# Attention with a split exponential: zeros counted by streaming time, doubled waves, GpSimd's lag in the plan, v in 22 columns

## The chip, the cores and the metric

The kernel runs on one core of a Trainium2 chip. A core has five engines that each run their own instruction list in order: TensorE (PE, matrix products), VectorE (DVE), ScalarE (ACT), GpSimd (POOL) and SyncE (SP, which starts transfers). They meet only at semaphores. TensorE writes its results to PSUM, in banks of 128 x 512 float32; everything else lies in SBUF. The metric is the device time of one execution in microseconds.

## The reference

Softmax attention over 32 heads of 2,048 rows and 20 columns, with normalised queries and keys and a temperature for each head:

```python
def reference(q, k, v, t):
    eps = 1e-6
    qn = q / (jnp.sqrt((q * q).sum(axis=-1, keepdims=True)) + eps)
    kn = k / (jnp.sqrt((k * k).sum(axis=-1, keepdims=True)) + eps)
    logits = jnp.einsum('bhqd,bhkd->bhqk', qn, kn) * t[None, :, None, None]
    attn = _softmax(logits, axis=-1)
    return jnp.einsum('bhqk,bhkd->bhqd', attn, v)
```

q, k and v are [1, 32, 2048, 20] in bf16, t is [32]. The logits are bounded by t, so the kernel takes no maximum: it sums exp(logit) times v and, in one more column of ones, exp(logit) itself, and divides at the end.

## The kernel before

**Tiling.** The heads are taken in 8 groups of 4 (`NH`), each head of a group in its own strip of 32 rows of TensorE. A group has 4 blocks of 512 queries (`QW`), so there are 32 blocks (`NSB`). In a block each of the 4 heads has 16 pieces of 128 keys: 64 units of 128 keys x 512 queries, 2,048 units in all. A unit is one matmul of kT against qT, an exponential of 128 x 512, and one or more matmuls of the result against v that add into `psO`, where head hh owns the partitions 32·hh to 32·hh + 31. Four heads use four strips, so up to four of these small matmuls run at once.

**Two paths for the exponential.** On the first path a wave of two units goes to one of two slots of `psA`, ScalarE computes exp on 128 x 1024 (L885), and each unit costs one product with v (`vaug`). On the second path a unit goes to one of three banks of `psD`. VectorE turns it into 16-bit integers that are the bits of an approximate power of two (`P1`, L325, into `dI`). Two more terms come from adding a constant to those integers: the shifts (`dS1`, `dS2`), on GpSimd (L338, two 16-bit numbers in one int32) or on VectorE (L340). The three terms, with the first one taken against v and also against half of v (`vhalf`, made at L345), cost four products with v. `dI` and `dS` are rings of 24 units (`RING`).

**The plan.** The order of all engines is written by a planner in Python when the kernel is built (`make_plan`). It steps through time in steps of 0.005 us, gives every operation a cost and a latency, and lets each engine take its next piece of work by rules. The result is a fixed list for each engine, with the waits that the data need. The rules that the change touches:

- `step_pe0` puts a wave on `psA` as soon as its slot is free, and with it a wave on `psD` if banks are empty (`step_qkd`). Between waves it does products with v (`pv_round`). `ALONE`, `DJOIN`, `PVHOLD` hold work back when a slot comes free soon. `D_WAIT` holds the second path when too many shifts wait; `D_END` and `D_LAST` end it near the end of the last block or move it on from the end of another.
- While `psO` of a finished block is being drained (VectorE transposes it to `accT`, L360), no product with v can be issued. In that time a wave is issued three times over, to the same place, if TensorE has been used too little (L875). Elsewhere `step_heat` adds a matmul of zeros into `psO` (L558, `HEATN` = 128 columns). "Used" is `in_use`: the share of the last `HEATW` us, weighted by the share of the four strips in use, against `HEAT`. At the very start `HEAT0` zero matmuls of 512 columns run (L562).
- `step_dve` picks VectorE's next operation by priority; two neighbouring conversions become one of 1024 columns if at least `JOINB` shifts wait. `shift_run` gives VectorE up to four shifts in one operation.
- `step_pool` gives GpSimd work that fits under an operation of VectorE that doesn't use the port that the two share (conversions, drains, reductions), with up to `POOL_MAX` shifts in one operation and `PSLACK` us of overrun. It makes GpSimd wait for the operation of VectorE before that one. `lock` keeps VectorE's port operations (shifts, squares, scalings, the half copy) back until GpSimd is done in the plan.
- Loads and transposing transfers go through SP's queue (`load_qk`, `load_v`, `tr_op`) with planned latencies. `PREP1` spreads the preparation of the second head group over time, `LOAD1` says when its loads may start, `PREPW` weighs GpSimd's operations in that spread.
- `zeros` fills the padding columns of `kpad`, `qpad` and `vaug` on GpSimd at the start. v has 20 columns, one of ones, and zeros up to 32.

## Time and profile before

| | us |
|---|---|
| median of 3 runs | 632.83 |
| lowest, highest | 632.67, 633.11 |
| the profiled execution's own time | 633.45 |
| its span, first to last instruction | 631.5 |

In the profile PE is TensorE's matmul, PEld its weight load, and each group of instructions has its line, engine, operation, `out<-in`, how often, then busy time in us, the mean of one in ns, and how long the engine sat idle just before such instructions with what ended that. Matmuls are pipelined and up to four run at once, so PE's busy share is no measure of how full TensorE is. Means of single operations include the tail that the next one overlaps. The granted clock of TensorE is given as a share of full speed; over the execution it averaged 0.995.

### The profile page before, as it was taken

What the parts mean: (1) busy time and instruction counts of PE and PEld (TensorE: products, weight loads), DVE (VectorE), ACT (ScalarE), POOL (GpSimd) and SP (SyncE); (2) the same over time, 40 slices, a digit from 0 to 9 for tenths busy, and PEclk for the clock granted to TensorE, in tenths of its full rate; (3) what the DMA queues carried; (4) which work ended last, traced back from release to release, by engine and by line L of the source; (5) the groups of instructions that cost most, each with busy time, mean ns of one, the idle gap of its engine ahead of it and who ended that gap; (6) DMA issues with size and microseconds to landing.
All of it is one profiled execution on the core that took longest, in us unless ns stands there. A gap on an engine that the chain in (4) does not pass through costs nothing.

```text
span 631.5 us, 15864 instructions
## 1 busy us (share of the span) xinstructions
PE 614.5 (97%) x6794; PEld 180.3 (29%) x6794; DVE 614.1 (97%) x869; ACT 618.8 (98%) x675; POOL 445.5 (71%) x491
## 2 busy tenths in 40 slices
PE   8999999999999999999999999999999999999996
PEld 4432222322222232223223222232222332222221
DVE  6999999999999999999999999999999999999995
ACT  6999999999999999999999999999999999999995
POOL 4586667766677776876768666776777777666772
PEclk8999999999999999999999999999999999999999
DMA  6610404041040130306031050400404022010000
GB/s 73 88 10 16 95 1 43 2 62 48 2 43 2 35 76 5 39 2 111 1 29 16 1 110 3 40 4 3 93 3 57 2 33 37 1 23 6 6 5 13
DMA packets 113772, 19.57 MB, mean 31 GB/s; under 512 B 102944, under 2 KB 113696, under 8 KB 113696
## 3 DMA queue, kind: packets, MB, share of 16 engines
q1 hardware_dynamic: 112896, 18.37, 19.9%
q8 instruction: 55, 0.90, 0.6%
q10 hardware_dynamic: 800, 0.12, 0.1%
q14 instruction: 21, 0.17, 0.1%
HBM read 7.87 MB, written 2.62 MB: 17 GB/s over the span
## 4 chain that ended last, share of the span: by engine, by line
ACT 72%; PE 26%; DVE 1%; DMA 0%; issue 0%; POOL 0%
ACT pA L885 72%; PE psO L714 12%; PE psA L692 10%; PE psD L692 2%; PE psO L558 2%; DMA qk<-in_q_dram 0%; DVE ssum L263 0%; POOL kpad L304 0%; DVE accT L360 0%; PE psD L570 0%; DVE sqs L260 0%; DVE ost L368 0%; DVE qT L585 0%; DVE rn L289 0%; DVE rec L364 0%
## 5 line engine op out<-in xcount | busy, mean ns | idle before, releaser
L885 ACT ACTIVATE pA<-psA 128x1024 f16<-128x1024 f32 (+1 forms) x667 | 614.5, 1111 | 2.0 <-PE psA L692 1.6
L338 POOL TENSOR_TENSOR dS<-dI,shc 128x256 int32<-128x256 int32 (+2 forms) x378 | 373.0, 1007 | 130.0 <-DVE dS L340 93.2
L325 DVE TENSOR_SCALAR dI<-psD 128x1024 int16<-128x1024 f32 (+1 forms) x486 | 434.1, 927 | 4.4 <-PE psD L692 1.8
L692 PE MATMUL psA<-qT,kT 32*128 32x512 bf16 x1553 | 283.0, 384 | 8.9 <-ACT pA L885 6.0
L714 PE MATMUL psO<-pA,vaug 128*32 128x512 f16 (+1 forms) x1333 | 233.7, 384 | 0.0
L714 PE MATMUL psO<-dS,vaug 128*32 128x512 f16 x1430 | 224.5, 385 | 0.0
L692 PE MATMUL psD<-qT,kT 32*128 32x512 bf16 x715 | 193.9, 383 | 0.0
L714 PE MATMUL psO<-dI,vaug 128*32 128x512 f16 x715 | 155.3, 386 | 0.0
L714 PE MATMUL psO<-dI,vhalf 128*32 128x512 f16 x715 | 152.0, 384 | 0.0
L692 PEld LDWEIGHTS psA<-qT,kT 32*128 32x128 bf16 x1553 | 69.0, 91 | 239.4 <-ACT pA L885 224.1
L340 DVE TENSOR_SCALAR dS<-dI 128x2048 int16<-128x2048 int16 (+2 forms) x182 | 122.5, 679 | 0.0
L714 PEld LDWEIGHTS psO<-dS,vaug 128*32 128x32 bf16 x1430 | 51.1, 94 | 73.2 <-issue 58.7
L714 PEld LDWEIGHTS psO<-pA,vaug 128*32 128x32 bf16 x1333 | 52.5, 94 | 37.5 <-issue 31.8
L692 PEld LDWEIGHTS psD<-qT,kT 32*128 32x128 bf16 x715 | 45.4, 91 | 22.1 <-DVE dI L325 10.2
L714 PEld LDWEIGHTS psO<-dI,vaug 128*32 128x32 bf16 x715 | 36.7, 93 | 24.5 <-issue 17.4
L714 PEld LDWEIGHTS psO<-dI,vhalf 128*32 128x32 bf16 x715 | 36.4, 94 | 22.0 <-issue 19.2
L366 POOL TENSOR_TENSOR ost<-accT,rec 128x320 bf16<-128x320 f32 x31 | 23.3, 753 | 16.7 <-DVE dS L340 9.5
L304 POOL TENSOR_TENSOR qpad<-qk,rn 128x320 bf16<-128x320 bf16 x31 | 22.0, 728 | 17.3 <-DVE dS L340 10.4
L558 PE MATMUL psO<-zt 128*128 128x128 bf16 x310 | 32.3, 228 | 0.1
L304 POOL TENSOR_TENSOR kpad<-qk,rn 128x320 bf16<-128x320 bf16 x31 | 22.2, 738 | 10.8 <-DVE dS L340 6.1
L558 PEld LDWEIGHTS psO<-zt 128*128 128x128 bf16 x310 | 19.7, 101 | 21.0 <-issue 20.1
L360 DVE STREAM_TRANSPOSE accT<-psO 128x512 f32<-128x512 f32 x32 | 22.6, 705 | 2.7 <-PE psO L714 2.7
(51 smaller groups left out, 100.1 us busy)
## 6 DMA issues: line engine op xcount, KB each, us to landing
vaug<-in_v_dram SPq DMA_DIRECT2D x32, 80.0 KB, 4.0
qk<-in_k_dram SPq DMA_DIRECT2D x7, 320.0 KB, 4.0
out_dram<-ost SPq DMA_DIRECT2D x28, 80.0 KB, 1.9
qk<-in_q_dram SPq DMA_DIRECT2D x6, 320.0 KB, 3.9
qk<-in_q_dram SPq DMA_DIRECT2D x4, 80.0 KB, 3.1
out_dram<-ost SPq DMA_DIRECT2D x7, 40.0 KB, 2.0
qk<-in_k_dram SPq DMA_DIRECT2D x1, 240.0 KB, 3.6
qk<-in_q_dram SPq DMA_DIRECT2D x1, 240.0 KB, 4.2
```

Of the source, the lines that this page charges most:

```text
L304: emit = lambda e, o=dst, x=src, s=sc: e.tensor_tensor(o, x, s, ALU.mult)
L325: lambda e: e.tensor_scalar(dst, psD[:, pb * QW:(pb + n) * QW], 1024.0 * LOG2E, 15360.0 - 1024.0 * LOG2K + SHIFTS[0], ALU.mult, ALU.add),
L338: lambda e: e.tensor_tensor(o.bitcast(I32), x.bitcast(I32), c, ALU.add), rd + ["shc"], wr)
L340: lambda e: e.tensor_single_scalar(o, x, float(SHIFTS[i] - SHIFTS[0]), ALU.add), rd, wr)
L360: dve("drain", QW, R1, lambda e: e.transpose(aT[:, :, :].rearrange("p b d -> p (b d)"), psO[:, :]), ["psO"], [("accT", b)], 0.03),
L366: pool_op("omul", 320, True, lambda e: e.tensor_tensor(dst, num, rcb, ALU.mult), [("accT", b), ("rec", b)], [("ost", ob, qg)]) if pool else
L558: return lambda e: e.matmul(bank, zt[:, 0:128], zt[:, 0:n], start=False, stop=False, skip_group_check=True)
L692: return lambda e: e.matmul(dst, lhsT, rhs, tile_position=(32 * hh, 0))
L714: return lambda e: e.matmul(dst, lhsT, rhs, start=first, stop=last, skip_group_check=True, tile_position=(0, 32 * hh))
L885: a = Op("ACT", "exp", lambda e, s=src, d=dst: e.activation(d, s, ACT.Exp), [("psA", slot)], [("pA", pslot, i) for i in range(WAVES[slot]) ...
```

## The change

Four things in the planner and one in the data, with new values for its constants:

- `in_use` is now the share of time in which any matmul streams, overlaps counted once. Zeros are added below `HEAT` = 0.7 of the last 1.7 us (before: 0.57 of strip-weighted use in 3.41 us). In a drain a wave is issued twice (`TWICE`), not three times, if the share is below `HEATQ` = 0.8. `HEAT0` is 13, and its first matmul now writes all of `psO`.
- GpSimd's operation under a VectorE operation is planned to start `PLAG` after the end of the VectorE operation before it, and the port is planned free `LOCKL` before its end. Up to four shifts in one operation.
- The latencies of the first loads (`LOAD0`) and of the transposing transfers (`TRL`, `TRK`) are longer in the plan.
- `vaug` and `vhalf` have 22 columns for each piece, not 32, and the products with v write 22 partitions of each strip.

```diff
-D_END = 6
-D_LAST = 18
-D_WAIT = 36
+VW = 22
+D_END = 2
+D_LAST = 14
+D_WAIT = 30
-PREPW = 0.3
-PREP1 = (.25,.35)
+PREPW = 0.2
+PREP1 = (.15,.45)
-DFIRST = 1
+DFIRST = 2
-JOINB = 8
-POOL_MAX = 3
-ALONE = (.2, 0)
+JOINB = 12
+POOL_MAX = 4
+ALONE = (.2,.2)
-PVHOLD = (.22,.22)
-HEAT0 = 11
+PVHOLD = (.25,.25)
+HEAT0 = 13
-HEAT = .57
-HEATW = 3.41
+HEAT = 0.7
+HEATQ = 0.8
+TWICE = 2
+HEATW = 1.7
+LOAD0 = 2.75
+TRL = 2.25
+TRK = 1.2
+PLAG = .03
+LOCKL = 0.12
-PSLACK = 0.15
+PSLACK = 0.3
-SOON = 8
+SOON = 1.2
-LOAD1 = 0.2
-DJOIN = 0.3
+LOAD1 = 0
+DJOIN = 0.4
...
-        vaug = [sbuf(f"vaug{i}", [128, NH, R, 32], BF16) for i in range(2)]
+        vaug = [sbuf(f"vaug{i}", [128, NH, R, VW], BF16) for i in range(2)]
...
-            return dve("vh", NH * R * 32, R4, lambda e: e.tensor_single_scalar(f(vpart[c]), f(vaug), c, ALU.mult),
+            return dve("vh", NH * R * VW, R4, lambda e: e.tensor_single_scalar(f(vpart[c]), f(vaug), c, ALU.mult),
...
-                        0.5, 4.0 if part != 0 else 2.2)]
+                        0.5, 4.0 if part != 0 else LOAD0)]
...
-                       [(which + "pad", b, r) for r in range(r0, r1)], keys, 0.58 + 0.17 * (r1 - r0), 1.75 + 0.17 * (r1 - r0))
+                       [(which + "pad", b, r) for r in range(r0, r1)], keys, 0.58 + 0.17 * (r1 - r0), TRL + 0.17 * (r1 - r0) + TRK * (hg == 0 and which == "k"))
...
-            o = Op("PE", "heat", None, ["zt"], [("psA", 0)])
+            o = Op("PE", "heat", None, ["zt"], [("psA", 0), "psO"])
...
                 for hh in strips:
                     s0 = max(st, grp[hh])
                     grp[hh] = s0 + TS
+                    used_w.append((s0, s0 + TS))
                     end = max(end, grp[hh])
...
-                used_w.append((st, end, 0.25 * TS * len(strips) / (end - st)))
...
-                dst = psO[32 * hh:32 * hh + 32, :]
+                dst = psO[32 * hh:32 * hh + VW, :]
...
-                return sum(max(0.0, min(b, now) - max(a, t0)) * c for a, b, c in used_w) / HEATW
+
+                x, u = t0, 0.0
+                for a, b in sorted(used_w):
+                    a, b = max(a, x), min(b, now)
+                    if b > a:
+                        u, x = u + b - a, b
+                return u / HEATW
...
-                        if cur > 0 and not cur_free() and in_use() < HEAT:
-                            mms, st_ = mms * 3, st_ * 3
+                        if cur > 0 and not cur_free() and in_use() < HEATQ:
+                            mms, st_ = mms * TWICE, st_ * TWICE
...
-                fits = lambda c: not busy or now + c <= end + PSLACK
+                st = max(now, on[-2].done + SEML + PLAG) if busy and len(on) > 1 else now
+                fits = lambda c: not busy or st + c <= end + PSLACK
...
-                finish(o, now, o.cost, o.lat)
-                free_["POOL"] = lock[0] = now + o.cost
+                finish(o, st, o.cost, o.lat)
+                free_["POOL"], lock[0] = st + o.cost, st + o.cost - LOCKL
```

More of the change, by code (lines that the diff above doesn't have):

```diff
@@ L178, in bass_standalone__qk_norm__prompt_kernel @@
         kT = [sbuf(f"kT{i}", [128, S], BF16) for i in range(2)]
-        vaug = [sbuf(f"vaug{i}", [128, NH, R, 32], BF16) for i in range(2)]
-        vpart = {c: [sbuf(f"v{n}{i}", [128, NH, R, 32], BF16) for i in range(2)] for c, n in ((.5, "half"),)}
+        vaug = [sbuf(f"vaug{i}", [128, NH, R, VW], BF16) for i in range(2)]
+        vpart = {c: [sbuf(f"v{n}{i}", [128, NH, R, VW], BF16) for i in range(2)] for c, n in ((.5, "half"),)}
         pA = sbuf("pA", [128, NPA // 2 * sum(WAVES) * QW], BF16)
@@ L501, in zeros @@
                 return [z(kpad[i][:, :, :, D:32], 0.0, "kz"), z(qpad[i][:, :, :, D:32], 0.0, "qz"),
-                        z(vaug[i][:, :, :, D:D + 1], 1.0, "vz"), z(vaug[i][:, :, :, D + 1:32], 0.0, "vz")]
+                        z(vaug[i][:, :, :, D:D + 1], 1.0, "vz"), z(vaug[i][:, :, :, D + 1:VW], 0.0, "vz")]
             pool_init(0.2, [Op("POOL", "iota", lambda e: e.iota(iot[:, :], [[-1, 128]], base=0, channel_multiplier=1,
@@ L558, in heat_mm @@
                 return lambda e: e.matmul(bank, zt[:, 0:128], zt[:, 0:n], start=False, stop=False, skip_group_check=True)
-            o = Op("PE", "heat", None, ["zt"], [("psA", 0)])
-            o.info = [(lambda e, i=i: e.matmul(psA[:, (i % 3) * QW:(i % 3 + 1) * QW], zt[:, 0:128], zt[:, :])) for i in range(HEAT0)]
+            o = Op("PE", "heat", None, ["zt"], [("psA", 0), "psO"])
+            o.info = [lambda e: e.matmul(psO[:, :], zt[:, 0:128], zt[:, :])] + [(lambda e, i=i: e.matmul(psA[:, (i % 3) * QW:(i % 3 + 1) * QW], zt[:, 0:128], zt[:, :])) for i in range(HEAT0 - 1)]
             P.link(o)
@@ L565, in make_plan @@
             free_["PE"] = 0.5 + 0.427 * HEAT0
-            used_w = [(0.0, 0.0, 0.0)]
+            used_w = [(0.0, 0.0)]
             psQ = psD[:, QW:2 * QW]
@@ L679, in pe_put @@
                 if st - used_w[0][0] > 20:
-                    del used_w[0:20]
-                used_w.append((st, end, 0.25 * TS * len(strips) / (end - st)))
+                    del used_w[0:40]
                 op.start, op.done = st, end + PEL
@@ L815, in step_heat @@
                 pe_mode, pe_t = "heat", st + 0.02
-                used_w.append((st, st + n, 1.0))
+                used_w.append((st, st + n))
                 op.start, op.done = st, st + n + PEL
```

## The prediction

> **What bounds the kernel now.** I read the page first: the shares of the engines, the chain that ended last, the costliest groups.
>
> ```profile
> span 631.5 us, 15864 instructions
> ...
> PE 614.5 (97%) x6794; PEld 180.3 (29%) x6794; DVE 614.1 (97%) x869; ACT 618.8 (98%) x675; POOL 445.5 (71%) x491
> ...
> ACT 72%; PE 26%; DVE 1%; DMA 0%; issue 0%; POOL 0%
> ...
> L885 ACT ACTIVATE pA<-psA 128x1024 f16<-128x1024 f32 (+1 forms) x667 | 614.5, 1111 | 2.0 <-PE psA L692 1.6
> L338 POOL TENSOR_TENSOR dS<-dI,shc 128x256 int32<-128x256 int32 (+2 forms) x378 | 373.0, 1007 | 130.0 <-DVE dS L340 93.2
> L325 DVE TENSOR_SCALAR dI<-psD 128x1024 int16<-128x1024 f32 (+1 forms) x486 | 434.1, 927 | 4.4 <-PE psD L692 1.8
> L692 PE MATMUL psA<-qT,kT 32*128 32x512 bf16 x1553 | 283.0, 384 | 8.9 <-ACT pA L885 6.0
> L692 PE MATMUL psD<-qT,kT 32*128 32x512 bf16 x715 | 193.9, 383 | 0.0
> L340 DVE TENSOR_SCALAR dS<-dI 128x2048 int16<-128x2048 int16 (+2 forms) x182 | 122.5, 679 | 0.0
> L558 PE MATMUL psO<-zt 128*128 128x128 bf16 x310 | 32.3, 228 | 0.1
> ```
>
> ScalarE's 667 exponentials take 614.5 us and were kept waiting 2.0 us in all. That is 0.921 us for a wave of two units, 0.461 us a unit. The rest of the span is the start and the tail, so a faster TensorE alone has next to nothing to give: what counts is how many of the 2,048 units go to ScalarE. Now 715 go the other way (the psD matmuls), over VectorE and GpSimd. The view of the middle by windows says whether VectorE has room for more (columns: window, length, then busy time of PE, PEld, DVE, ACT, POOL, the granted clock, the DMA share, GB/s):
>
> ```profile
> 20.00:620.00 600.00, 591.63 (x6584) 169.87 (x6583) 595.82 (x818) 599.38 (x651) 436.20 (x474) 1.00 0.20 30
> ```
>
> It has not: VectorE idles 4.2 us of 600 and ScalarE 0.6 us. Two engines share the work and both are full, so a gain must come from VectorE time that falls away or goes to GpSimd, or from the two ends.
>
> **The exchange rate.** A unit on the second path costs VectorE 434.1/715 = 0.607 us for its conversion and 122.5/715 = 0.171 us for its share of the shifts, 0.778 us in all. If F us of VectorE time come free, x more units go there with 0.778x + 0.461x = F, and the time falls by 0.461x = 0.37 F. If both shifts of the added units fall on VectorE the rate is 0.33. I use 0.35. One unit that changes sides for any other reason is worth 0.46 us.
>
> **GpSimd's runs (POOL_MAX 3 to 4, PSLACK, PLAG, LOCKL).** By shape, and one cycle in order of time (start, length), with a place where GpSimd ran late:
>
> ```profile
> L325 DVE TENSOR_SCALAR dI<-psD 128x1024 int16<-128x1024 f32 x229 | 277.2, 1211 | 2.6 <-PE psD L692 1.3 <-PE psA L692 0.5
> L325 DVE TENSOR_SCALAR dI<-psD 128x512 int16<-128x512 f32 x257 | 171.7, 674 | 1.8 <-PE psO L558 0.8 <-PE psD L692 0.5
> L340 DVE TENSOR_SCALAR dS<-dI 128x2048 int16<-128x2048 int16 x165 | 114.3, 697 | 0.0
> L340 DVE TENSOR_SCALAR dS<-dI 128x1536 int16<-128x1536 int16 x9 | 5.2, 577 | 0.0
> L340 DVE TENSOR_SCALAR dS<-dI 128x1024 int16<-128x1024 int16 x8 | 3.4, 428 | 0.0
> L338 POOL TENSOR_TENSOR dS<-dI,shc 128x768 int32<-128x768 int32 x113 | 165.2, 1466 | 70.8 <-DVE dS L340 45.6 <-DVE sqs L260 9.7 <-DVE rsb L283 2.5
> L338 POOL TENSOR_TENSOR dS<-dI,shc 128x512 int32<-128x512 int32 x123 | 127.7, 1039 | 47.9 <-DVE dS L340 39.5 <-DVE vhalf L345 2.4 <-DVE sqs L260 1.8
> L338 POOL TENSOR_TENSOR dS<-dI,shc 128x256 int32<-128x256 int32 x142 | 85.7, 612 | 11.3 <-DVE dS L340 8.1 <-DVE ssum L286 1.2 <-DVE ssum L285 1.0
> ...
> 299.53 1.81 DVE L325 TENSOR_SCALAR dI<-psD 128x1024 int16<-128x1024 f32 x2
> 299.69 1.47 POOL L338 TENSOR_TENSOR dS<-dI,shc 128x768 int32<-128x768 int32 x1 [0.72 <-DVE dS L340]
> 301.26 0.68 DVE L340 TENSOR_SCALAR dS<-dI 128x2048 int16<-128x2048 int16 x1
> ...
> 265.34 2.61 POOL L338 TENSOR_TENSOR dS<-dI,shc 128x768 int32<-128x768 int32 x3
> 267.61 0.89 DVE L340 TENSOR_SCALAR dS<-dI 128x2048 int16<-128x2048 int16 x1
> ```
>
> GpSimd does 3·113 + 2·123 + 142 = 727 shift units at 373.0/727 = 0.513 us. VectorE does 4·165 + 3·9 + 2·8 = 703 at 122.5/703 = 0.174 us. GpSimd's ops cost 0.185 us fixed and 0.427 us a unit (612, 1039, 1466 ns), so a run of four would take 1.89 us. Half of the runs of two and three grown by one unit, instead of a new op for it, is 118 · 0.185 = 21.8 us of GpSimd, 42 shift units, 7.4 us of VectorE, -2.6 us of time. The other end is the port. GpSimd starts 0.16 us after the conversion that covers it, so a run of four ends at 2.05 us, where VectorE wants its own shift at 1.73. At 267.61 GpSimd's run lasted 0.34 us into VectorE's op, which took 0.89 us, not 0.68: 0.21 us lost. Against 0.174 us that the moved unit saves, 113 such runs lose 113 · 0.04 = 4 us, +1.4 us. I take **-1.8**, nearer the gain, since cover longer than three units pays no such wait.
>
> The Trainium skill (SBUF — State Buffer, "SBUF: two separate sides") says that the port pair that VectorE and GpSimd share is an exclusive lock and that the loser blocks for the whole of the other's instruction. By it the run of four would hold VectorE 0.32 us and 113 of them would cost 113 · 0.146 = 16 us, +5.8 us in place of my -1.8. The row has 0.21 us lost for 0.34 of overlap: a wait, but shorter than the rule has it.
>
> PLAG and LOCKL put the 0.16 us lag and the early release into the plan. VectorE's runs of four average 697 ns against 680 undisturbed, 165 · 0.017 = 2.8 us that a truer plan could save. Ends: -1.0 and, if ops are only planned later, +1.0. I take **-0.3**.
>
> **Joined conversions (JOINB 8 to 12).** Two single ones take 2 · 674 = 1348 ns on paper, less the 0.075 us by which the 1211 and the 674 overlap in the 1.81 above: 62 ns more than a joined one. All 229 lost is 14 us of VectorE, +5.0 us; none is 0. The bar matters only while few shifts wait. I take a tenth, 1.4 us: **+0.5**.
>
> **Second-path waves held back (D_WAIT 30, ALONE, DJOIN, PVHOLD).** These let fewer psD waves out at a time. What is queued behind is VectorE's next conversion. TensorE's psD matmuls keep it 1.8 us now. Nothing hides more of that, since VectorE is full. Doubling or ending it is ±0.6. I take **+0.4**; the far case is a rival.
>
> **The start (HEAT0, zeros, LOAD0, TRL, TRK, PREP1, LOAD1).** In order of time, and by windows of PE alone (busy, clock):
>
> ```profile
> 1.19 4.19 PE L562 MATMUL psA<-zt 128*128 128x512 bf16 x11 [1.19 <-DVE act_scr L509]
> ...
> 8.30 2.53 PE L558 MATMUL psO<-zt 128*128 128x128 bf16 x22
> ...
> 10.76 0.61 PE L692 MATMUL psA<-qT,kT 32*128 32x512 bf16 x2
> ...
> 11.41 5.61 ACT L885 ACTIVATE pA<-psA 128x1024 f16<-128x1024 f32 x6 [1.08 <-PE psA L692]
> ...
> 14.72 0.69 DVE L610 CAST kT<-psD 128x512 bf16<-128x512 f32 x1 [2.32 <-PE psD L604]
> ...
> 20.60 3.62 DVE L325 TENSOR_SCALAR dI<-psD 128x512 int16<-128x512 f32 x5 [0.81 <-PE psO L558]
> ...
> 4.56:7.97 3.41, 1.70 (x16) 1.00 1.02 111
> 7.97:11.38 3.41, 3.41 (x30) 0.50 0.85 50
> 158.14:161.55 3.41, 3.19 (x22) 1.00 0.00 0
> ...
> 400.47:403.88 3.41, 3.05 (x30) 1.00 0.55 33
> ```
>
> TensorE was busy 1.70 of 3.41 us, the clock fell to half for the next 3.41 us, and 22 zeros took 2.53 us at 0.115 us each; the third wave stood behind them and ScalarE lost 1.08 us. The first burst of 11 zeros takes 0.38 us each; two more add at most 0.76 us to the first stretch; zeros counted by streaming over 1.7 us fill less of a gap in one go. Ends: 0, if the clock falls again with the same number of zeros, and -1.1. I exclude a loss: the burst ends at 5.38, and 1.71 us of the stretch to 7.97 were idle. I take **-0.6**. VectorE's waits of 2.32 and 0.81 us come from TensorE's fixed order against planned loads. With the loads planned later they could go (3.13 · 0.35 = -1.1) or grow as much: **-0.3**.
>
> **v in 22 columns.**
>
> ```profile
> L345 DVE TENSOR_SCALAR vhalf<-vaug 128x2048 bf16<-128x2048 bf16 x8 | 5.5, 681 | 0.0
> ...
> L714 PEld LDWEIGHTS psO<-dS,vaug 128*32 128x32 bf16 x1430 | 51.1, 94 | 73.2 <-issue 58.7
> L692 PEld LDWEIGHTS psD<-qT,kT 32*128 32x128 bf16 x715 | 45.4, 91 | 22.1 <-DVE dI L325 10.2
> ```
>
> The half copy shrinks from 2048 to 1408 elements. 2048 against 1024 is 697 against 428 ns above, so 640 fewer are 0.17 us, eight times 1.3 us of VectorE: **-0.45**, other end 0. A weight load of 32 columns takes what one of 128 takes, so 22 give TensorE nothing. v's loads hide behind a whole head group (no DMA in the chain); without that cover they would cost their landing.
>
> **Doubled waves, zeros in the middle, the tail.** 1553 - 1333 = 220 extra matmuls are 55 tripled waves; doubling leaves 110. ScalarE's waits outside the start are 2.0 - 1.4 = 0.6 us at most: **-0.2**. Zeros: 32.3 us of an engine off the path, 0, ±0.3. D_END and D_LAST let up to four more units of the last block go over VectorE: -1.8 at best, +1.2 if a late shift and its matmuls come after the last exponential. VectorE sits idle 2.65 us there:
>
> ```profile
> 625.85 0.72 DVE L360 STREAM_TRANSPOSE accT<-psO 128x512 f32<-128x512 f32 x1 [2.65 <-PE psO L714]
> ```
>
> I take **-0.3**. SOON and PREPW only reorder the same operations: 0, within the ends of the others.
>
> **Sum.** -1.8 - 0.3 + 0.5 + 0.4 - 0.6 - 0.3 - 0.45 - 0.2 - 0.3 = -3.05 us. The profiled execution took 633.45 us (631.5 span and 1.95 around it), 0.62 above the median of 632.83. 630.4 in its terms, **629.8** as a median. Its own range is 627 to 632.
>
> **The rivals.** *GpSimd takes far more.* It waits 93.2 us behind VectorE's shifts, and each one moved shortens that. If 140 units move, VectorE saves 140 · 0.174 = 24 us: -8.5, with the ends 622. Against it: in the cycle above GpSimd already fills 1.63 of 1.73 us. *Nothing net.* The plan settles on the same split and gains at the start are lost in the joins: 632.8. *Slower: the second path is starved.* Place: TensorE's order, psD waves held for ScalarE's next slot or for the backlog. Price: 0.46 us a unit. From 7 units lost (3.05/0.46) the gain is gone; 715 to 700 is +6.9, less 2 for the ends and v: 637.5. For it: three edits hold and VectorE has no slack. Against: VectorE has shifts to do meanwhile. *Slower: the clock falls in the drains.* A tripled wave made double streams 0.21 us less; two in a stretch of 3.05 to 3.19 us leave about 2.6, and between 1.70 (fell) and 3.05 (held) nothing is known. Each fall cost ScalarE 1.08 us above; in a quarter of the 32 drains that is +8.6 on the forecast, 638.5.
>
> The Trainium skill (TensorE: Matmul & The Clock Gate, "Why this matters for your kernels") asks only that no idle gap pass about 3 us. By that rule the drains stay safe and this last rival falls away; the trace disagrees, since the clock fell after a stretch that was half busy.
>
> **The numbers.** Forecast 0.43, GpSimd far more 0.17, nothing net 0.12, starved 0.20, clock 0.08. The range of 8 in 10 cuts the outer parts of the second and the last two: 622 to 638.5. A measurement here tells 0.2% (1.3 us) from no change. Faster takes 0.40 of the forecast and all of the second, 0.57; within 0.2%, 0.11, the no-net case mostly; slower 0.32.
>
> **What would show it.** Exponentials: 667 down to about 663 or fewer, psD matmuls above 715, at 0.92 us a wave. GpSimd runs of 128x1024, more than 727 units there, and VectorE's 128x2048 mean under 0.72 us. Joined conversions near 205. No 1.08 us wait at 11 us. Clock 1.00 in all windows past 20 us. The forecast is wrong if psD matmuls fall below 715, if VectorE shows idle time in the middle, or if the clock falls in a drain.

## The result, and the profile after

The changed kernel takes 634.64 us in the median of 14 executions (632.49 to 640.89), the kernel before 632.67 us (14, 631.93 to 633.62) beside it: a ratio of 1.0046, 95% interval 1.0025 to 1.0067. It is slower, by 2 us, where 629.8 was forecast.

The 14 times are two groups. Seven lie between 632.49 and 633.26 us with a mean granted clock of 0.997 to 0.999, seven between 636.02 and 640.89 us with 0.979 to 0.991. No execution of before in that comparison took more than 633.62. So there are two questions: why do executions whose clock holds gain nothing, and why does the clock fall in the others?

The page of after and its middle by windows, an execution of the first group (632.73 us):

```profile
span 630.9 us, 15786 instructions
...
ACT 92%; PE 5%; SPq 1%; DMA 1%; DVE 1%; issue 0%
...
L900 ACT ACTIVATE pA<-psA 128x1024 f16<-128x1024 f32 (+1 forms) x668 | 612.5, 1171 | 1.2 <-PE psA L701 0.7
L334 DVE TENSOR_SCALAR dI<-psD 128x512 int16<-128x512 f32 (+1 forms) x519 | 434.7, 874 | 5.4 <-PE psD L701 3.1
L701 PE MATMUL psD<-qT,kT 32*128 32x512 bf16 x713 | 197.1, 383 | 1.2 <-DVE dI L334 1.2
```

```profile
20.00:620.00 600.00, 584.95 (x6538) 158.39 (x6536) 595.25 (x838) 599.22 (x655) 452.81 (x457) 1.00 0.18 29
```

The exponentials went up by one, 667 to 668, the psD units down, 715 to 713. VectorE is as full as before (595.25 of 600 us, 595.82 before). The chain of waits is ScalarE for 92%, before for 72%: TensorE hands it its waves in time now.

**ScalarE's gain.** The unbroken trains of exponentials in the timeline of ScalarE (start, length, count, wait in front), before and then after:

```profile
11.41 451.00 ACT L885 ACTIVATE pA<-psA 128x1024 f16<-128x1024 f32 x489 [1.08 <-PE psA L692]
462.56 162.02 ACT L885 ACTIVATE pA<-psA 128x1024 f16<-128x1024 f32 x176 [0.16 <-PE psA L692]
```

```profile
8.62 3.77 ACT L900 ACTIVATE pA<-psA 128x1024 bf16<-128x1024 f32 x4 [0.19 <-PE psA L701]
12.65 9.40 ACT L900 ACTIVATE pA<-psA 128x1024 f16<-128x1024 f32 x10 [0.26 <-PE psA L701]
22.61 29.44 ACT L900 ACTIVATE pA<-psA 128x1024 f16<-128x1024 f32 x32 [0.56 <-PE psD L701]
52.27 569.85 ACT L900 ACTIVATE pA<-psA 128x1024 f16<-128x1024 f32 x622 [0.22 <-PE psA L701]
```

Before, 451.00/489 = 0.922 us lie between two exponentials; after, 569.85/622 = 0.916. The trains are called unbroken because the next exponential comes before the last has run out (one takes more than 1.1 us, overlapped). An exponential that starts late by less than that overlap leaves no idle time, and the delay stands as busy time. From its first start to its last end ScalarE takes 624.58 - 8.39 = 616.19 us before and 622.12 - 8.62 = 613.50 after, with one wave more: 3.6 us less at the same number of waves. The waits between the trains are about equal (1.24 us before, 1.04 after), so the gain lies within the trains.

**Where it went.** The first exponential starts 0.23 us later. One more wave is 0.92. The rest goes into the tail, the time from the last exponential to the last transposition of psO. TensorE's products with v in just that time (window, length, busy, count, clock), before and after:

```profile
624.58:625.85 1.27, 1.21 (x24) 1.00 0.06 13
```

```profile
622.12:625.18 3.06, 3.02 (x49) 1.00 0.06 11
```

When ScalarE ends, 49 matmul records are still to come, not 24, and TensorE runs them back to back: 1.27 us became 3.06. Together -3.6 + 0.23 + 0.92 + 1.79 = -0.7 us, the 0.6 by which the span shrank.

The profiled execution of before is one of its longer ones, however. Its wait of 1.08 us comes from a fall of the clock at the start (the 0.50 at 7.97 in the prediction's windows), and its mean clock is 0.995. Of the 105 executions of before beside the experiments below, 19 have a mean clock of 0.994 to 0.996, and they take about 1 us more than the 85 at 0.997 or above. e12 below has the same first instructions and shows the usual start (windows of PE: busy, clock):

```profile
4.56:7.97 3.41, 2.25 (x16) 1.00 1.03 115
7.97:11.38 3.41, 3.23 (x41) 1.00 0.84 50
```

Against such an execution of before nothing is gained: the seven undisturbed times of the changed kernel, those whose clock holds, have a median of 632.83 us, before has 632.67.

**The hole at 21 us.** SyncE's queue after, then before, and the landing time of one transposition in after's view of transfers:

```profile
8.97 1.30 SPq L404 DMA_DIRECT2D qk<-in_k_dram  x1
10.31 0.51 SPq L404 DMA_DIRECT2D qk<-in_q_dram  x1
11.81 6.12 SPq L414 DMA_DIRECT2D vaug<-in_v_dram  x4
17.98 1.99 SPq L423 DMA_TRANSPOSE kT<-kpad  x1
```

```profile
13.69 1.37 SPq L414 DMA_TRANSPOSE kT<-kpad  x1
...
23.69 0.90 SPq L395 DMA_DIRECT2D qk<-in_k_dram  x1
```

```profile
kT<-kpad SPq DMA_TRANSPOSE x1, 4.0
```

With `LOAD1` = 0 the second head group's loads go out at once, and the four for v hold the queue from 11.81 to 17.93. The first group's transposition of kT, issued at 13.69 before, stands behind them until 17.98 and lands 4.0 us later. A further execution of the changed kernel (a0 below) shows who waits for it, and what the clock then does (a row of PE, then windows of PE: busy, clock); behind it after's own row and window at that place:

```profile
21.89 0.37 PE L701 MATMUL psD<-qT,kT 32*128 32x512 bf16 x1 [0.43 <-DMA kT<-kpad]
```

```profile
17.81:21.22 3.41, 3.41 (x44) 1.00 0.83 103
21.22:24.64 3.42, 2.92 (x27) 1.00 0.26 52
24.64:34.88 10.24, 10.24 (x69) 0.50 0.20 23
```

```profile
22.16 0.37 PE L701 MATMUL psD<-qT,kT 32*128 32x512 bf16 x1 [1.17 <-DVE dI L334]
```

```profile
21.46:24.87 3.41, 2.71 (x27) 1.00 0.60 114
```

In after the hole is 1.17 us long, and the trace names VectorE's conversion, which ended at 22.05, as what ended it; the transposition had landed at 21.98 (17.98 + 4.0), so TensorE would have stood for it until about then in any case. The clock fell to half for 10.24 us in a0 after a window with 0.50 us of idle time, and it held in after, where that window has 0.70. The clock's records change in steps of 3.41 us, with boundaries at 21.22 in a0 and about 21.4 in after, so the hole ends 0.7 to 0.8 us behind a boundary in both. Neither its length nor its place tells the two apart.

### The profile page after: what moved, and what is told of

It is laid out like the page before. It is cut to its first block, busy times and chain, and to the rows that moved or that the text cites. A ratio compares the mean times of both kernels' runs of the same rounds, so it can differ in the third digit from the quotient of the medians.

```text
span 630.9 us, 15786 instructions
## 1 busy us (share of the span) xinstructions
PE 606.5 (96%) x6752; PEld 168.5 (27%) x6752; DVE 614.1 (97%) x891; ACT 616.7 (98%) x676; POOL 462.0 (73%) x474
## 4 chain that ended last, share of the span: by engine, by line
ACT 92%; PE 5%; SPq 1%; DMA 1%; DVE 1%; issue 0%
ACT pA L900 92%; PE psO L723 2%; PE psA L701 2%; SPq L414 1%; DMA vaug<-in_v_dram 1%; PE psO L567 1%; DVE dI L334 0%; PE psD L701 0%; SPq L404 0%; DVE accT L369 0%; DVE ost L377 0%; SPq L538 0%; DVE rec L373 0%; PE psD L613 0%
## 5 line engine op out<-in xcount | busy, mean ns | idle before, releaser
L347 POOL TENSOR_TENSOR dS<-dI,shc 128x512 int32<-128x512 int32 (+3 forms) x361 | 390.2, 1095 | 116.8 <-DVE dS L349 76.3
L334 DVE TENSOR_SCALAR dI<-psD 128x512 int16<-128x512 f32 (+1 forms) x519 | 434.7, 874 | 5.4 <-PE psD L701 3.1
L723 PE MATMUL psO<-pA,vaug 128*22 128x512 f16 (+1 forms) x1335 | 242.9, 383 | 0.6 <-DMA vaug<-in_v_dram 0.6
L723 PE MATMUL psO<-dS,vaug 128*22 128x512 f16 x1426 | 234.8, 383 | 0.0
L723 PE MATMUL psO<-dI,vaug 128*22 128x512 f16 x713 | 159.8, 383 | 0.2 <-DVE accT L369 0.2
L723 PE MATMUL psO<-dI,vhalf 128*22 128x512 f16 x713 | 157.1, 382 | 0.0
L349 DVE TENSOR_SCALAR dS<-dI 128x2048 int16<-128x2048 int16 (+3 forms) x171 | 120.0, 714 | 0.0
L723 PEld LDWEIGHTS psO<-dS,vaug 128*22 128x22 bf16 x1426 | 50.5, 89 | 72.6 <-issue 61.2
L723 PEld LDWEIGHTS psO<-pA,vaug 128*22 128x22 bf16 x1335 | 50.2, 89 | 35.0 <-issue 30.1
L723 PEld LDWEIGHTS psO<-dI,vaug 128*22 128x22 bf16 x713 | 35.7, 89 | 24.8 <-issue 15.4
```

What stands on the lines that cost most here:

```text
L334: lambda e: e.tensor_scalar(dst, psD[:, pb * QW:(pb + n) * QW], 1024.0 * LOG2E, 15360.0 - 1024.0 * LOG2K + SHIFTS[0], ALU.mult, ALU.add),
L347: lambda e: e.tensor_tensor(o.bitcast(I32), x.bitcast(I32), c, ALU.add), rd + ["shc"], wr)
L349: lambda e: e.tensor_single_scalar(o, x, float(SHIFTS[i] - SHIFTS[0]), ALU.add), rd, wr)
L723: return lambda e: e.matmul(dst, lhsT, rhs, start=first, stop=last, skip_group_check=True, tile_position=(0, 32 * hh))
```

## The experiments

All times are medians on one chip in one comparison. "Fell" is said of an execution with a mean clock of 0.992 or less; a single fall of 3.41 us, as in the profile of before (0.995), is not counted. Of before, 1 execution of 105 in these comparisons fell.

**a0: the changed kernel once more,** with the next comparisons.

> The changed kernel once more, on the chip of the other runs of this call. Theory A: the executions fall in two kinds again, at 632.5 to 634 us with a clock of 0.997 or more and at 636 and over with 0.992 or less, and the profile of one of the second kind has its half-clock stretch begin right after a window that holds the hole at 20.8 to 22.2 us or the wait for v at 11 us.

635.89 us (11 executions), ratio 1.0031, interval 1.0011 to 1.0052; 6 fell, the other five took 632.23 to 633.18. Both groups are there again, and in its profile the hole is where the clock falls.

**e1: 20 zeros in front of the wait for kT,** after's order kept.

```diff
...
+            i = next((i for i, o in enumerate(pe) if any(d.name == "Tk" and d.eng == "SP" for d in o.deps)), None)
...
+                pe[i - 1].info = pe[i - 1].info + [heat_mm(psO[:, 0:HEATN], HEATN)] * 20
```

> The changed kernel with its order kept, and 20 zeros of 128 columns (1.1 us) more behind the product with v after which TensorE stood idle from 20.8 to 22.2 us. Theory A (the clock falls because the first group's transposing transfer of k comes late and leaves that hole, and whether it falls depends on how a window of 3.41 us lies over it): all executions at 632.5 to 633.3 us with a clock of 0.997 or more, none at 636 or 640. Theory B (the clock falls in the drains with doubled waves): still about half of them at 636 to 641 with clocks of 0.98 to 0.99. Theory C (spread from elsewhere): as B.

639.04 us (7), ratio 1.0072, 1.0035 to 1.0109; 5 fell. Its profile is that of the longest, 649.58 us. The hole at 21 us is gone there, and the clock falls at two other places, earlier behind the wait for v and in the middle (all engines' busy time in the order PE, PEld, DVE, ACT, POOL, then the clock):

```profile
13.33:30.40 17.07, 17.07 (x121) 8.23 (x118) 6.92 (x18) 10.48 (x11) 3.85 (x5) 0.50 0.58 72
...
364.90:368.32 3.42, 3.09 (x26) 1.09 (x26) 3.40 (x5) 3.42 (x5) 3.42 (x7) 1.00 0.00 0
368.32:392.21 23.89, 23.62 (x153) 4.92 (x153) 15.80 (x22) 16.66 (x18) 11.53 (x16) 0.50 0.12 23
```

Once fallen the clock stays low for five and seven windows, and ScalarE works 10.48 of 17.07 and 16.66 of 23.89 us: 6.6 and 7.2 us lost. The second fall comes after a window with 0.33 us of idle time, 16 us behind a drain and 10 us ahead of the next. One hole isn't the only cause.

**e2: the drains' waves three times over in after's order.**

```diff
-                            mms, st_ = mms * TWICE, st_ * TWICE
+                            mms, st_ = mms * 3, st_ * TWICE
```

> The changed kernel with its order kept, but every doubled wave of a drain issued a third time. Theory A (hole at 21 us): still about half of the executions at 636 to 641 us with clocks of 0.98 to 0.99. Theory B (drains): all at 632.5 to 633.5 us with clocks of 0.997 or more.

637.77 us (6), ratio 1.0081, 1.0059 to 1.0103; 2 fell, and the other four took 636.96 to 637.9, against 632.2 to 633.3 with doubled waves. So the tripling costs 4 to 5 us with no fall counted. Its last train has the same 622 exponentials as that of after:

```profile
57.92 573.50 ACT L900 ACTIVATE pA<-psA 128x1024 f16<-128x1024 f32 x622 [0.33 <-PE psA L701]
```

573.50 against 569.85 us: 3.65 us inside a train that shows no idle time. And its clock falls in the profile at the hole at 21 us too: doubling in the drains didn't cause that.

**e3 and e4: `LOAD1` undone in after, and put alone into before.**

```diff
-LOAD1 = 0
+LOAD1 = 0.2
```

> The changed kernel with LOAD1 back at 0.2, so that the second group's loads go behind the first group's transposing transfers in SP's queue; the rest of the plan is made anew. Theory A: the transposing transfer of k issues near 14 us instead of 18, no hole at 21 us, all executions within 0.2% of one another with clocks of 0.997 or more, at 630 to 633 us. Theory B: about half still 3 to 8 us longer.

> The kernel before with LOAD1 = 0 alone. Theory A: the transposing transfer of k issues near 18 us, TensorE has a hole of about 1 us near 21 us, and some executions are 3 to 8 us longer with clocks under 0.992. Theory B (doubled waves are needed): all executions within 0.3% of 632.7 us.

e3: 634.04 us (12), ratio 1.0013, 0.9995 to 1.0032; 10 of 12 at 633.76 to 634.15, 2 fell. The transposition goes out at 14.05 again, TensorE is busy for all of 21.2 to 24.6 us, and the falls drop from 13 of 25 executions (after and a0) to 2 of 12, and to 5 of 35 with e6, e8 and e9 below, which have `LOAD1` undone too; the new plan has a tail of 4.3 us. e4: 641.6 us (6), ratio 1.0155, 1.0122 to 1.0188; 5 of 6 fell, where before hardly ever does. New plans alone don't do that: e7, e11, e14, e17 and e18 below, planned anew with before's loads, have no fall in 38 executions, e13 and e15 3 in 24. With before at 633.12 beside it, e4 lost 3.5 us without a fall (636.64) and 8.5 in the median; what the new plan costs by itself lies in both. In the profile of the execution without a fall ScalarE waits 1.24 us behind the hole, and the tail of 2.90 us is 1.6 longer than before's. The clock held there although the window at the hole (the second view) has only 2.25 us of work:

```profile
22.80 54.52 ACT L885 ACTIVATE pA<-psA 128x1024 f16<-128x1024 f32 x59 [1.24 <-PE psD L692]
```

```profile
21.19:24.60 3.41, 2.25 (x25) 1.00 0.66 128
```

**e5 and e6: zeros in both holes of the start,** at the wait for v and at that for kT, in after (e5); at the wait for v alone, with `LOAD1` undone (e6).

```diff
+            def fill(i, n):
...
+                z.info = [heat_mm(psO[:, 0:HEATN], HEATN)] * n
+                pe.insert(i, z)
...
+                    fill(next(i for i, o in enumerate(pe) if o.name == "PV"), 20)
...
+                    fill(next(i for i, o in enumerate(pe) if any(d.name == "Tk" and d.eng == "SP" for d in o.deps)), 20)
```

> The changed kernel with its order kept, and 20 zeros of 128 columns (1.1 us) in each of two holes at the start: before the first product with v (where TensorE waited 0.6 to 1.25 us for v's load), and before the wave that waits for the first group's transposing transfer of k (1.2 us). Theory A2 (the clock falls only where one of these two holes takes the streaming share of a window under about 0.4): no window at half clock before the tail, executions at 632.5 to 634 us with at most one in seven longer. Theory B (anywhere in the span): still half of the executions 3 us or more longer.

> The changed kernel with LOAD1 back at 0.2 (the second hole gone) and 20 zeros before the first product with v (the first hole filled). Theory A2: no execution more than 0.4% over the fastest, level as the undisturbed ones of the run with LOAD1 alone put back, 633.8 to 634.1 on that chip, 0.1 to 0.2% over the kernel before. Theory B: outliers remain.

e5: 633.73 us (12), ratio 1.0044, 1.0016 to 1.0073; 3 fell. e6: 634.56 us (6), ratio 1.0040, 1.0026 to 1.0054; 1 fell. Filling the holes of the start doesn't end the falls, and 3 of 12 against 13 of 25 is too few to say that it makes them rarer. What causes the others stays open.

**e8: runs of three on GpSimd,** in e3's kernel.

```diff
-POOL_MAX = 4
+POOL_MAX = 3
```

> The changed kernel with LOAD1 at 0.2 and POOL_MAX back at 3. If the runs of four shifts pay their own port wait (the measured 740 ns of VectorE's runs of four against 697 before), that mean falls to about 700 ns, GpSimd does some 730 units instead of 770, and the undisturbed time stays within 0.2% of the run with LOAD1 alone put back. If the runs of four were a net gain, it is over 0.2% longer.

636.55 us (6), ratio 1.0087, 1.0062 to 1.0111: 2.5 us over e3, with 726 units on GpSimd, 670 waves (e3: 668) and a tail of 5.4 us (4.3). Read alone, runs of four are worth 2.5 us. e14, e17 and e18 show what such a reading is worth. VectorE's runs of four shifts take 706 ns here, against 735 in e3:

```profile
L349 DVE TENSOR_SCALAR dS<-dI 128x2048 int16<-128x2048 int16 x167 | 116.5, 706 | 0.0
```

**e9: `D_END` and `D_LAST` as before,** in e3's kernel.

```diff
-D_END = 2
-D_LAST = 14
+D_END = 6
+D_LAST = 18
```

> The changed kernel with LOAD1 back at 0.2 and D_END, D_LAST back at 6 and 18. Theory T (the undisturbed gain of the doubled waves is given back in the tail, because more units of the last block go over the second path and their products with v are still due when the last exponential is done): the final transposition of psO starts at most 2 us after the last exponential ends, against 4.3 us with LOAD1 alone put back, and the undisturbed time falls from 0.15% over the kernel before to 0.2 to 0.4% under it. Rival (the tail is set by the order of the products, not by the last block's share): tail and time as with LOAD1 alone put back.

633.95 us (11), ratio 1.0025, 1.0015 to 1.0036, a tail of 4.25 us, in e3 4.32. Bringing the two constants back doesn't bring back the short tail.

**e11 and e12: doubled waves alone in before,** planned anew (e11), and with before's order kept (e12): the plan counts three, two are issued.

```diff
-                            mms, st_ = mms * 3, st_ * 3
+                            mms, st_ = mms * 2, st_ * 3
```

> The kernel before with every drain's wave issued twice instead of three times, nothing else. Theory D (the third issue makes ScalarE late by 0.1 us in each of some 30 drains, hidden in its busy time): the intervals of 1.02 us between exponentials vanish, 3 us less; some of it is given back, since the plan now gives ScalarE 669 waves, not 667 (+1.8 us): 631 to 632 us where the kernel before has 632.7. My forecast's view (ScalarE's waits are all in the idle column, at most 0.6 us): 632.5 to 634. Theory B for the clock: with doubled waves some executions now fall to a clock under 0.992.

> The kernel before with its order kept: the 55 waves that its plan issues three times over in the drains are issued twice, nothing is planned anew. Theory A: the 0.1 us that each of the late exponentials loses is a pure loss; without it ScalarE's 4.4 us of late starts shrink to about 0.4 us and the end comes 3 to 4 us earlier, 629 us, a ratio of 0.994 to 0.996. Rival B: VectorE idles only 4 us in the middle, its list is unchanged, and TensorE's fixed order makes ScalarE wait behind conversions and shifts; the late starts vanish from the drains and come back as waits elsewhere or in the tail: 631.5 to 632.7 us.

e11 (with `st_ * 2`): 632.79 us (11), ratio 1.0002, 0.9993 to 1.0011. e12: **629.04 us** (6, 628.86 to 629.29), ratio 0.9940, 0.9927 to 0.9954, none fell. Its whole exponential stretch, from the timeline of ScalarE, and its tail:

```profile
8.19 611.47 ACT L885 ACTIVATE pA<-psA 128x1024 bf16<-128x1024 f32 x667 [0.19 <-PE psA L692]
```

```profile
619.66:620.98 1.32, 1.26 (x24) 1.00 0.05 12
```

One train of 667 at 0.917 us each, and 24 matmuls left at its end, as before. Planned anew, e11 has the even exponentials too, but 669 waves, and this tail:

```profile
622.23:625.32 3.09, 3.05 (x45) 1.00 0.03 5
```

Two waves more (1.84 us) and 1.77 us of tail make 3.6 of the 3.75 us between the two kernels. The doubling is worth 3.6 us (3.5 against the executions of before with a clock of 0.997 or more), and the new plan gives all of it back.

**e7: v in 22 columns alone in before** (with the first zero matmul over all of `psO`), planned anew.

```diff
+VW = 22
...
-        vaug = [sbuf(f"vaug{i}", [128, NH, R, 32], BF16) for i in range(2)]
+        vaug = [sbuf(f"vaug{i}", [128, NH, R, VW], BF16) for i in range(2)]
...
```

> The kernel before with v in 22 columns and the first zero matmul over all of psO, nothing else. By the forecast's term 0.45 us less, 632.3 where the kernel before has 632.7; the plan is made anew, so another order may cost or gain up to 2 us by itself. Theory of no effect: within 0.2%.

634.97 us (6), ratio 1.0036, 1.0023 to 1.0048; none fell. An edit that was to save VectorE's time, and does (the half copy took 620 ns for 681), made the kernel 2.3 us slower; the tail is 3.1 us.

**e13: the rule for zeros and drains alone in before.**

```diff
-HEAT = .57
-HEATW = 3.41
+HEAT = 0.7
+HEATQ = 0.8
+TWICE = 2
+HEATW = 1.7
...
```

> The kernel before with the rule for zeros and drains of the changed kernel alone (share of streaming over 1.7 us, below 0.7 for zeros and below 0.8 for a wave issued twice), first burst of zeros, loads, GpSimd and v as before. Theory A: the rule by itself leaves stretches in which the clock falls; a quarter of the executions or more show a clock below 0.993 and take 636 us or more. Rival B: the falls need the hole that the early loads make; nearly all executions have a clock of 0.995 or more, and the time is that of the doubled waves in the plan of before, 632 to 633.5 us.

633.18 us (12), ratio 1.0014, 0.9991 to 1.0036; 2 of 12 fell, and the lowest five took 632.13 to 632.42. The rule alone gives e11's time, and a fall now and then that e11 (0 of 11) doesn't have. 2 of 12 is too few to call the rule the cause.

**e14 and e15: GpSimd's part alone in before,** with the drains three times over (e14) and twice (e15).

```diff
-POOL_MAX = 3
+POOL_MAX = 4
...
+PLAG = .03
+LOCKL = 0.12
...
-PSLACK = 0.15
+PSLACK = 0.3
...
-                fits = lambda c: not busy or now + c <= end + PSLACK
+                st = max(now, on[-2].done + SEML + PLAG) if busy and len(on) > 1 else now
+                fits = lambda c: not busy or st + c <= end + PSLACK
...
-                finish(o, now, o.cost, o.lat)
-                free_["POOL"] = lock[0] = now + o.cost
+                finish(o, st, o.cost, o.lat)
+                free_["POOL"], lock[0] = st + o.cost, st + o.cost - LOCKL
```

> The kernel before with GpSimd's part of the change alone: runs of up to four shifts, the planned lag of 0.03 us behind VectorE's operation, the port planned free 0.12 us early, 0.3 us of overrun. Theory A: this part is worth what the prediction gave it, 2.1 us, and what the runs of four were worth in the plan of after (2.5 us): 630.2 to 630.7 us, GpSimd at 760 units or more. Rival B: the units that GpSimd takes from VectorE come back as a longer tail, as the gain of the doubled waves did: 632 to 633.5 us with more than 2 us between the last exponential and the last transposition.

> The kernel before with GpSimd's part of the change and the waves of the drains issued twice, loads, zeros, constants of the end and v as before: the parts of the change that do something, without those that cost. If the two parts add up, 2 us from GpSimd and 0 to 3 from the doubled waves: 628 to 631 us with a clock of 0.995 or more in every execution. If the end swallows them, 632 to 633.5 us with a tail of 3 us or more. If the falls of the clock need no early loads, some executions at 636 us or more.

e14: 635.15 us (6), ratio 1.0039, 1.0024 to 1.0053, with 742 units on GpSimd, psD at 713 and a tail of 2.5 us. e15: 632.47 us (12), ratio 1.0002, 0.9989 to 1.0016; 1 fell. Doubling gains 2.7 us here; GpSimd's part brings nothing that can be seen in either plan.

**e16: the drains' waves once,** before's order kept.

```diff
-                            mms, st_ = mms * 3, st_ * 3
+                            mms, st_ = mms * 1, st_ * 3
```

> The kernel before with its order kept and the 55 waves of the drains issued once. Theory A: the repeats are needed for the clock; without them TensorE streams too little in the drains and the clock falls in some of them, at 1 us or more each: 632 to 640 us, scattered. Rival B: the clock holds without them and ScalarE, already without late starts when they are issued twice, gains nothing more: 628.5 to 629.3 us.

630.9 us (9, 628.32 to 633.92), ratio 0.9969, 0.9947 to 0.9991; 3 fell, and three at 628.3 to 628.9 did not lose anything. Its profile has four falls in drains. One, by windows of PE:

```profile
136.81:140.22 3.41, 2.60 (x23) 1.00 0.72 137
140.22:143.63 3.41, 3.41 (x30) 0.50 0.78 209
143.63:147.04 3.41, 3.41 (x46) 1.00 0.02 5
```

The execution took about 5 us more than the undisturbed ones, some 1.25 us a fall. So the repeats are needed for the clock, and two are enough: e11 and e12 have 17 executions without a fall.

**e17 and e18: before with a plan disturbed by 0.002 us** and nothing else.

```diff
-PEL = .17
+PEL = .172
```

```diff
-ACT1 = .24
+ACT1 = .242
```

> The kernel before, planned anew with one latency of TensorE in the plan longer by 0.002 us (0.17 to 0.172) and nothing else changed. Theory A: every new plan draws another tail and another split, and that of before was a lucky one: the time moves by 1 to 3 us, mostly up (633.5 to 636), with a tail over 2 us or more than 667 waves. Rival B: the planner is steady, and what the plans of the changed kernels lost comes from their rules: within 0.6 us of 632.6.

> The kernel before, planned anew with one latency of ScalarE in the plan longer by 0.002 us (0.24 to 0.242) and nothing else changed. Theory A: as above, a time 1 to 3 us off, mostly up (633.5 to 636). Rival B: within 0.6 us of 632.6.

e17: 633.62 us (9), ratio 1.0018, 1.0007 to 1.0028. e18: 634.33 us (6), ratio 1.0032, 1.0019 to 1.0044. Neither change has a meaning, and they cost 0.9 and 1.6 us. The end of e18, from its timeline:

```profile
537.73 85.63 ACT L885 ACTIVATE pA<-psA 128x1024 f16<-128x1024 f32 x93 [0.16 <-PE psA L692]
```

```profile
626.75 0.72 DVE L360 STREAM_TRANSPOSE accT<-psO 128x512 f32<-128x512 f32 x1 [4.41 <-PE psO L714]
```

The last exponential ends at 623.36 and the transposition starts at 626.75: a tail of 3.4 us from a constant that moved by 0.002. e17 keeps the tail of 1.27 us; there the trains lose more, 613.93 us for 665 exponentials where before has 613.02.

The kernels beside each other (the profiled execution of each; the last column is the median in its own comparison, where before has 632.6 to 632.8):

| kernel | drains | waves | tail, us | us |
|---|---|---|---|---|
| before | x3 | 667 | 1.27 | 632.7 |
| e17 | x3, new plan | 667 | 1.27 | 633.62 |
| e18 | x3, new plan | 666 | 3.39 | 634.33 |
| e7 | x3, new plan | 666 | 3.13 | 634.97 |
| e14 | x3, new plan | 668 | 2.49 | 635.15 |
| e15 | x2, new plan | 670 | 2.75 | 632.47 |
| e11 | x2, new plan | 669 | 3.09 | 632.79 |
| after, clock held | x2, new plan | 668 | 3.06 | 632.5 to 633.3 |
| e12 | x2, before's plan | 667 | 1.32 | 629.04 |

Four new plans with tripled drains take 633.6 to 635.2 us (that of e4 636.6 without a fall), before 632.7: its plan is the best drawn so far. With the order kept doubling is worth 3.6 us (e12 to before) and 4 to 5 (after to e2), planned anew 2.7 (e15 to e14). A new plan plus doubling comes out where before was. Why the new plans leave a longer tail, and what rule of the planner would end it, stays open: e7, e14 and e18 have tails of 2.5 to 3.4 us with `D_END` and `D_LAST` as before, and the windows show only that TensorE has the products left over.

## Why the prediction was wrong

**The step that failed most: "the start ... I exclude a loss".** The exclusion covered the burst of zeros, and there it was right: in the profile of after 19 zeros took 1.24 us at the full clock, the third wave came at 9.70 us, and the wait of 1.08 us is gone. But `LOAD1` stood in the heading of that paragraph and got no term. Its transfers moved ahead of the transposition in SyncE's queue. e4, with that edit alone, lost 3.5 us without a fall and 8.5 in the median, the cost of its new plan included. In after and a0 13 of 25 executions fell and lost 3 to 8 us, one of them 22; with `LOAD1` undone 5 of 35 fell. How a hole leads to a fall in one execution and not in the next stays open.

Of the 4.8 us between the forecast of 629.8 and the 634.64 measured, 1.8 are these falls. The other 3.0 are a gain that the undisturbed executions (632.83) don't have either.

**The start's own term, -0.6.** It was priced at a fall that the profiled execution of before has and most others, by their times and clocks, don't, so the median had little of it to lose. Eight profiles with before's first zeros (e4, e7, e11, e12, e14, e15, e16, e18) have no such fall; before, e13 and e17 have one, with waits of ScalarE of 1.08, 0.76 and 1.08 us.

**Doubled waves: -0.2 forecast, -3.6 measured (e12).** The term was bounded by ScalarE's idle column, "2.0 - 1.4 = 0.6 us at most". The column has no room for an exponential that comes late while the last one is still ending. The distance of 0.922 us from one to the next could be read in before's timeline; that ScalarE can do 0.917 came with e12. 665 times 0.005 is 3.3 us. The mechanism, that a third issue keeps ScalarE waiting, was right, and its size was wrong.

**The sum itself.** It added terms as if the plan stayed and each edit moved a few units at 0.46 us. Every new plan draws its tail and its split again. e17 and e18 show 0.9 and 1.6 us for 0.002 us of planned time, more than any term of the sum but one. The tail's term, -0.3 by `D_END` and `D_LAST`, came out as +1.8, and tails of 2.5 to 3.4 us stand in plans that left those two alone (e7, e14, e18). Of v in 22 columns, at -0.45, e7 shows only the new plan (+2.3); the half copy itself went from 681 to 604 ns in after, 0.6 us over eight, not 1.3 (in e3, at 522 ns, it is the 1.3).

**GpSimd's runs: the mechanism right, the worth not shown.** The conversions of two units and the shifts in after, by shape:

```profile
L334 DVE TENSOR_SCALAR dI<-psD 128x1024 int16<-128x1024 f32 x194 | 234.8, 1210 | 1.9 <-PE psD L701 0.9 <-PE psA L701 0.2
...
L347 POOL TENSOR_TENSOR dS<-dI,shc 128x512 int32<-128x512 int32 x126 | 130.6, 1038 | 44.4 <-DVE dS L349 34.4 <-DVE sqs L269 5.3 <-DVE rsb L292 1.1
L347 POOL TENSOR_TENSOR dS<-dI,shc 128x1024 int32<-128x1024 int32 x61 | 115.2, 1891 | 34.0 <-DVE dS L349 28.6 <-DVE sqs L269 1.4 <-DVE rsa L297 1.1
L349 DVE TENSOR_SCALAR dS<-dI 128x2048 int16<-128x2048 int16 x157 | 114.7, 740 | 0.0
L347 POOL TENSOR_TENSOR dS<-dI,shc 128x256 int32<-128x256 int32 x124 | 74.8, 611 | 16.5 <-DVE rsb L292 3.9 <-DVE dI L334 2.2 <-DVE sqs L269 1.7
L347 POOL TENSOR_TENSOR dS<-dI,shc 128x768 int32<-128x768 int32 x50 | 73.2, 1464 | 21.8 <-DVE dS L349 12.7 <-DVE sqs L269 3.5 <-DVE rsa L297 2.1
```

A run of four takes 1.891 us (1.89 was the estimate), and GpSimd does 4·61 + 3·50 + 2·126 + 124 = 770 units, 43 more, about the 42 expected. VectorE's runs of four rose from 697 to 740 ns, where the prediction wanted them under 720. A place in after (start, length) shows the overlap at the port:

```profile
616.45 1.89 POOL L347 TENSOR_TENSOR dS<-dI,shc 128x1024 int32<-128x1024 int32 x1 [0.63 <-DVE dS L349]
618.08 0.81 DVE L349 TENSOR_SCALAR dS<-dI 128x2048 int16<-128x2048 int16 x1
...
620.55 0.68 DVE L349 TENSOR_SCALAR dS<-dI 128x2048 int16<-128x2048 int16 x1
```

GpSimd's run of four ends 0.26 us behind the start of VectorE's shifts, which take 0.81 us, not 0.68; and with runs of three the mean falls back to 706 ns (e8). That is 157 · 0.043 = 6.8 us, against 47 units fewer at 0.174, 8.2 us. What is left, 1.4 us of VectorE, is worth 0.5 us by the rate of 0.35, not the 1.8 and 0.3 of the two terms. In e14 and e15 it isn't seen; e8's 2.5 us lies within what plans differ by.

**Joins and held waves** were sized well: 194 joined conversions (205 expected), 35 fewer at 62 ns, 2.2 us of VectorE, +0.8; its waits for psD went from 1.8 to 3.1 us, +0.5.

**The rivals.** "Nothing net" is what the undisturbed executions do, though for the reason above and not for a plan that settles on the same split. "The clock falls in the drains" had the mechanism and the price (1.08 us a fall forecast, some 1.25 in e16), but the place was wrong: in no profile with doubled drains does a fall begin in one. It falls at the holes of the start, where it stayed down for 10.24 us and not for one window, and in e1 once in the middle of a block. "Starved" didn't happen: psD lost 2 units, not 15. Nor did "GpSimd takes far more": 43 units moved, not 140.

By the Trainium skill's gap rule, as the prediction quotes it, the hole couldn't matter: 0.43 us is far below 3. The Trainium skill has a second rule, which the prediction missed (TensorE: Matmul & The Clock Gate, "A second HAM failure mode: psum-queue depth-cycling"): in another kernel frequent small idle times between groups of matmuls made the clock swing. The trace agrees in that short idle times were enough, 0.50 us in the window of a0 and 0.81 in that of e16; it doesn't show that they must be many, since 0.43 of a0's 0.50 us are one wait.

## What to carry to other kernels

Where an order is planned by a program, price an edit with the order kept (change what is issued, not what is planned) and measure how far the time moves by a meaningless change of the plan; no term below that spread can be forecast or tested by planning anew. Read the distance from one instruction to the next on the engine that bounds, not its idle column. Before a wait is priced from a profile, compare that execution's time and clock with the others: the 1.08 us here stood in the profiled execution and not in most. For every constant that moves a transfer, list what stands behind it in the queue.

## What the runs showed of the hardware

TensorE's clock falls after stretches that are mostly busy: 3.09 us of 3.42 with a matmul in flight in e1 and 2.92 in a0, 2.60 of 3.41 in e16, while 2.71 held in after and 2.25 in e4. The busy time of a window therefore doesn't decide it; what does stays open, and the same kernel falls in one execution and not in the next. At the start the traces give a hint. The clock is granted in steps of 3.41 us whose beginning differs from execution to execution. In the three profiles with the fall at the start it first became full 4.5 to 4.6 us into the span, in the eight without it at 4.1 or at 5.5 to 7.1 us. Eleven profiles don't prove it, but the place of the steps against the work fits as the cause of that fall. At the hole at 21 us it isn't enough: with 4.2 us in a0 the clock fell, with 4.1 in e4 and 4.3 in after it held.

Once down it stayed for 3.41 us in the drains of e16, and for 10.24, 13.65, 17.07 and 23.89 us in a0, e2 and e1: three, four, five and seven steps.
